# A one-core FFT filter plus gated MLP: the layout of the normalised rows, one low op for two, and ten opening pieces on GpSimd

## The chip, the cores and the metric

The kernel runs on one core of a Trainium2 chip. The metric is the device time of one execution in microseconds, given as the median of several runs. A separate profiled execution gives the trace.

## The reference

The input x has 2048 rows of 448 numbers. It is normalised row by row, and two branches of the normalised xn are added to x:

```python
xn = _layernorm(x, axis=-1)
return x + _A_ref(xn, A_w_r, A_w_i) + _B_ref(xn, B_W_gate, B_W_up, B_W_down)
...
# _A_ref: a filter in the frequency plane
X = rfft2(x) * (w_r + 1j * w_i);  y = irfft2(X, s=(S, D))
# _B_ref: a gated MLP with 1792 hidden units
gate = x @ W_gate;  up = x @ W_up;  gate = gate * (gate > 0)
return (gate * up) @ W_down
```

## The kernel before

**Numbers.** Every matmul operand is split into a float16 high half and a float16 low half (the value minus the high half). A product takes three passes: high by high, high by low, low by high. A "low op" is the subtraction that makes a low half; it reads two tensors of SBUF (the value and its high half).

**Rows.** The rows are taken as 16 tiles n2 = 0..15 of 128 rows. Four chunks q hold the tiles with n2 % 4 = q and are worked in the order 0, 2, 1, 3. A tile goes through these steps, and the opening calls them by these short names: `lx` loads it (L220), `st` takes its statistics on VectorE (L248, L251), `sq` and `rs` make the reciprocal deviation for a group of tiles (L259 to L273), `xn` normalises it in float32 on VectorE (L291), `hi` rounds it to float16 on ScalarE (L298 from x in chunk 0, L300 from xn in the others), `lo` subtracts (L320, L321), `cp` and `cl` make small copies inside the tile on GpSimd (L304 and L305 for the high half, L309 and L310 for the low half). The tile in SBUF is `tt`, nine blocks of 128 columns; there are four such buffers, taken in turn.

**Layout.** The columns of a row are split by their remainder mod 4 into three groups a, b, c (of 112, each filled up to 128 with 16 of the odd group) and d, the 64 odd columns left. In `tt` they stand as a, b, c, d high, then d, a, b, c low, then two blocks of copies that hold the whole odd group (48 + 16 zeros + 64) for the Fourier part, high and low.

**Transposition.** The blocks must be transposed into `T`. For chunk 0 TensorE does it (`tpA`, `tpB`, L335) and VectorE or ScalarE copies the result out of PSUM (`vevA`, `aevA` and so on, L343 and L341); block 8 alone goes by a DMA transpose (`dt`, L329). For chunk 2 whole tiles go by DMA transposes (`dm`, L329). All DMA issues named here stand in SyncE's queue.

**Weights.** A hidden slab f (128 units; 14 in three groups) has a gate and an up slab g = 0, 1. `lw` loads one (L226), `wsq` squares it on ScalarE (L186), `par` sums over partitions on GpSimd (L189), `wsc` makes a scale on VectorE (L192, L196), `whi` makes its high half on ScalarE (L665) and `wlo` its low half on VectorE (L669).

**MLP.** `gu` is one slab's passes over 512 rows (L715). The last d block needs only 64 rows of the array, so two slabs share four half passes, `hp` (L722). `re` and `tm` make relu and product from PSUM (L752 on ScalarE, L756 on VectorE), `gh` and `gl` split it (L760, L764). The down projection is L783. In chunk 0 slab 0 is split further into pieces `hh`, `lh`, `hl` by half of the rows, so that TensorE can start early. `kw` and `warm` are dummy matmuls (L1023).

**Order.** For the opening (the first 38 us or so) the order of all engines is written out by hand in the string `OPENING`: 230 pieces; each engine runs its own pieces in that order. It ends with the last slab of chunk 0 and `hp4`, the half passes that also open chunk 2. Behind it the order comes from a planner: background work is dealt out between the units of the MLP by costs written in the code, and the framework places the instructions.

Of the kernel before, what the change touches and what calls it, by code (L numbers as in the profile page):

```python
# [133 lines left out]
def tile_gfnet_reglu(ctx: ExitStack, tc: tile.TileContext, x, xr, wgu, wd, wf, wrow, ident, c_fd, c_fm, c_im, c_row, c_id,  # L134
                     out):
    nc = tc.nc
# [8 lines left out]
    def fx():  # L145
        return psum.tile([128, 512], F32, name="fx", bufs=2)
# [131 lines left out]
    xn, tt, xn_b = {}, {}, {}  # L278
    tts = [ft([128, 9, 128], F16, f"tt{i}") for i in range(4)]
    for t in tts:  # L280
        G.memset(t[:, 7:9, 48:64], 0.0)

    def new_tt(n2):
        tt[n2] = tts[state.setdefault("tn", 0) % 4]
        state["tn"] += 1

    def ln_xn(n2):
        xn_b[n2] = free.pop(0)
        xn[n2] = xn_b[n2].rearrange("p g c k -> p (g c k)")[:, 0:D]
        r, _, mean = rsn[n2 % 4, n2 // 4]  # L290
        V.tensor_scalar(xn[n2], xr_t[n2], mean, r, op0=OP.subtract, op1=OP.mult)  # L291

    def ln_hi(n2, fused=False):
        new_tt(n2)
        o = tt[n2].rearrange("p a b -> p (a b)")[:, 0:D]
        r, nm, _ = rsn[n2 % 4, n2 // 4]
        if fused:
            A.activation(o, xr_t[n2], AF.Identity, scale=r, bias=nm)  # L298
        else:
            A.activation(o, xn[n2], AF.Copy)  # L300

    def ln_copy(n2):
        t = tt[n2]
        G.tensor_copy(t[:, 7, 0:48].rearrange("p (a b) -> p a b", b=16), t[:, 0:3, 112:128])  # L304
        G.tensor_copy(t[:, 7, 64:128], t[:, 3, 0:64])  # L305

    def ln_copy_lo(n2):
        t = tt[n2]
        G.tensor_copy(t[:, 8, 0:48].rearrange("p (a b) -> p a b", b=16), t[:, 4:7, 112:128])  # L309
        G.tensor_copy(t[:, 8, 64:128], t[:, 3, 64:128])  # L310
# [6 lines left out]

    def ln_lo(n2):
        x, t = xn[n2], tt[n2].rearrange("p a b -> p (a b)")
        V.tensor_tensor(t[:, 512:896], x[:, 0:384], t[:, 0:384], op=OP.subtract)  # L320
        V.tensor_tensor(t[:, 448:512], x[:, 384:448], t[:, 384:448], op=OP.subtract)  # L321
        free.append(xn_b.pop(n2))

    tp, last = {}, {}

    def ln_dma(n2, a=0):
        q, j = n2 % 4, n2 // 4
        o = Tq[q][:, a:9, 128 * j:128 * (j + 1)]
        last["S"] = nc.sync.dma_start_transpose(o, tt[n2][:, a:9].rearrange("p a b -> p (a b)")).ins  # L329

    def ln_tp(n2, tiles):
        if n2 not in tp:
            tp[n2] = fx().bitcast(F16).rearrange("p (a b) -> p a b", b=128)
        for a in tiles:
            P.transpose(tp[n2][:, a, :], tt[n2][:, a, :], id_t)  # L335

    def ln_ev(n2, a0, a1, act):
        q, j = n2 % 4, n2 // 4
        o = Tq[q][:, a0:a1, 128 * j:128 * (j + 1)]
        if act:  # L340
            last["A"] = A.activation(o, tp[n2][:, a0:a1], AF.Copy).ins  # L341
        else:
            last["V"] = V.tensor_copy(o, tp[n2][:, a0:a1]).ins  # L343
# [359 lines left out]

    hps, ht = {}, {}

    SEQ = [(r + 4 * k, r) for r in range(3) for k in (0, 1)] + [(t, 4 + t) for t in range(3)] + [(3, 3)]
    TOP = ((slice(0, 64), 3), (slice(64, 128), 7))

    def gu_open(f, q):
        hps[f, q] = psum.tile([128, 2, 512], F32, name="gu", bufs=2)  # L710
# [44 lines left out]
        g1 = g1s[f, q]  # L755
        last["V"] = V.scalar_tensor_tensor(g1, hps[f, q][:, 1, :], 2.0 ** -22, g1, op0=OP.mult, op1=OP.mult).ins  # L756
# [443 lines left out]
```

## Time and profile before

| | |
|---|---|
| median of 3 runs | 446.72 us (446.71 to 446.97) |
| profiled execution | 446.92 us, span 445.1 us |
| TensorE busy | 438.4 us, 98% |
| VectorE busy | 373.5 us, 84% |
| ScalarE busy | 178.9 us, 40% |
| GpSimd busy | 32.9 us, 7% |
| granted TensorE clock | 1.00 in every stretch |

In the profile PE is TensorE's matmuls, PEld its weight loads, DVE VectorE, ACT ScalarE, POOL GpSimd, and SPq SyncE's queue that issues DMAs. A row of the timeline gives the start, the duration, the engine, the line, the operation, output and input, how many instructions are merged, and in brackets the idle time before it with what ended it. Instructions of one engine overlap by a little, so a step from start to start is shorter than the duration. Grouped rows give count, busy time and the mean in ns.

### The profile page before, as it was taken

To read this page: it belongs to the slowest core of one execution; us is meant where nothing else is said; L and a number is where in the kernel's file an instruction comes from. 1 tells how busy PE (TensorE), PEld (TensorE's weight loads), DVE (VectorE), ACT (ScalarE), POOL (GpSimd) and SP (SyncE) were. 2 spreads that over 40 slices of the span, in tenths; PEclk is the share of its full clock that TensorE was granted. 3 is DMA by queue.
4 is the path that set the end of the run, shared out by engine and by line. 5 is a ranking of instruction groups with operands and counts; after the bars stand their busy time and mean duration, and the time that the engine had idled before them with its cause. 6 is when DMAs were issued, how large, how long until landed. Compare 5 with 4: busy or idle time off the path is not lost.

```text
span 445.1 us, 7091 instructions
## 1 busy us (share of the span) xinstructions
PE 438.4 (98%) x2630; PEld 218.8 (49%) x2630; DVE 373.5 (84%) x802; ACT 178.9 (40%) x365; POOL 32.9 (7%) x97
## 2 busy tenths in 40 slices
PE   8999999999999999999999999999999999999997
PEld 3543554444546444444444444444444455556565
DVE  5988696998858979999999999896997997766364
ACT  5886252351543666043233145344142242233230
POOL 2431031040000120000000010000000000000000
DMA  8929966041001261432220021000001333231113
GB/s 271 323 52 282 371 217 119 1 90 41 0 14 61 95 222 34 133 105 62 85 80 6 1 84 55 0 13 0 14 0 42 93 96 90 55 96 34 63 43 124
DMA packets 37115, 39.72 MB, mean 89 GB/s; under 512 B 17927, under 2 KB 32473, under 8 KB 37081
## 3 DMA queue, kind: packets, MB, share of 16 engines
q1 hardware_dynamic: 35928, 37.40, 27.4%
q10 hardware_dynamic: 1152, 1.87, 2.1%
q8 instruction: 20, 0.33, 0.3%
q14 instruction: 15, 0.11, 0.1%
HBM read 24.45 MB, written 3.67 MB: 63 GB/s over the span
## 4 chain that ended last, share of the span: by engine, by line
PE 91%; DVE 3%; DMA 2%; ACT 1%; issue 1%; POOL 1%; SPq 0%; ACTq 0%
PE gu L715 50%; PE dn L783 29%; PE gu L722 3%; PE fx L611 2%; PE fx L357 2%; PE fx L632 2%; PE fx L389 2%; DMA y<-in_xr 1%; DMA T<-tt 1%; DVE bst L248 1%; DVE wt L669 1%; DVE y L291 0%; DVE g L756 0%; ACT T L341 0%; DVE tt L320 0%
## 5 line engine op out<-in xcount | busy, mean ns | idle before, releaser
L715 PE MATMUL gu<-T,wt 128*128 128x512 f16 (+1 forms) x1140 | 256.1, 375 | 0.0
L715 PEld LDWEIGHTS <-wt 128*128 128x128 f16 x1140 | 108.7, 98 | 129.8 <-issue 9.3
L783 PE MATMUL dn<-wdt,h 128*128 128x448 f16 (+2 forms) x684 | 136.4, 349 | 0.0
L783 PEld LDWEIGHTS <-h 128*128 128x128 f16 x684 | 65.8, 98 | 59.9
L752 ACT ACTIVATE g<-gu 128x512 f32<-128x512 f32 x56 | 33.2, 594 | 115.1 <-PE gu L722 77.4
L760 ACT ACTIVATE h<-g 128x512 f16<-128x512 f32 x56 | 35.0, 627 | 47.3 <-DVE g L756 47.3
L756 DVE SCALAR_TENSOR_TENSOR g<-gu,g 128x512 f32<-128x512 f32 x56 | 38.5, 687 | 11.4 <-ACT g L752 11.3
L790 DVE SCALAR_TENSOR_TENSOR xy<-dn,dsc,xy 128x448 f32<-128x448 f32 (+2 forms) x49 | 32.9, 671 | 15.1 <-PE dn L783 14.8
L764 DVE TENSOR_TENSOR h<-g,h 128x512 f16<-128x512 f32 x56 | 38.5, 689 | 4.9 <-ACT h L760 4.8
L665 ACT ACTIVATE wt<-wst,wsc 128x512 f16<-128x512 f32 x28 | 19.1, 716 | 15.7 <-DVE wsc L196 15.7
L669 DVE SCALAR_TENSOR_TENSOR wt<-wst,wsc,wt 128x512 f16<-128x512 f32 x28 | 20.5, 749 | 0.0
L637 DVE SCALAR_TENSOR_TENSOR xy<-fx,fsc,xy 128x448 f32<-128x448 f32 x16 | 10.8, 681 | 10.7 <-PE fx L632 10.7
L189 POOL PARTITION_ALL_REDUCE wm<-wm x15 | 7.8, 521 | 158.9 <-ACT junk L186 158.9
L396 DVE TENSOR_TENSOR y<-y 128x456 f32<-128x456 f32 x22 | 13.9, 631 | 4.8 <-DMA row<-y 4.5
L722 PE MATMUL gu<-T,wt 64*128 64x512 f16 x112 | 17.0, 381 | 0.8 <-DMA T<-tt 0.7
L186 ACT ACTIVATE junk<-wst 128x512 bf16<-128x512 f32 x28 | 17.4, 622 | 0.2
L595 ACT ACTIVATE vt<-y,fsc 128x912 f16<-128x912 f32 x8 | 8.4, 1052 | 20.7 <-PE fx L611 12.3
L618 ACT ACTIVATE wf<-fx 114x512 f16<-114x512 f32 x16 | 9.4, 588 | 17.4 <-PE fx L611 16.6
L553 DVE TENSOR_TENSOR y<-y,sw 128x456 f32<-128x456 f32 x16 | 10.1, 628 | 5.7 <-DMA sw<-y 5.7
L395 DVE TENSOR_TENSOR y<-y 128x456 f32<-128x456 f32 x22 | 13.8, 628 | 0.2
L611 PEld LDWEIGHTS <-vt 128*128 128x128 f16 x192 | 12.0, 98 | 3.3
L611 PE MATMUL fx<-wf,vt 128*128 128x128 f16 x192 | 13.2, 219 | 0.0
(115 smaller groups left out, 431.4 us busy)
## 6 DMA issues: line engine op xcount, KB each, us to landing
wst<-in_wgu SPq DMA_DIRECT2D x28, 256.0 KB
wf<-in_wf SPq DMA_DIRECT2D x8, 456.0 KB
sw<-y SPq DMA_DIRECT2D x16, 224.4 KB
y<-in_xr SPq DMA_DIRECT2D x16, 224.0 KB
xy<-in_x SPq DMA_DIRECT2D x16, 224.0 KB
out<-xy SPq DMA_DIRECT2D x15, 224.0 KB
wdst<-in_wd SPq DMA_DIRECT2D x14, 224.0 KB
sw<-y SPq DMA_DIRECT2D x8, 228.0 KB
```

Source lines behind the costliest of these rows:

```text
L186: A.activation(o, src, AF.Square, scale=SQ, accum_out=acc)
L611: P.matmul(o, v[:, h, w], m[:, c, :], start=(i == 0), stop=(i == 2), skip_group_check=True)
L665: A.activation(w[:, 0:4, :], wst[f, g], AF.Copy, scale=wsc[f, g])
L669: V.scalar_tensor_tensor(w[:, 4:8, :], st, sc, w[:, 0:4, :], op0=OP.mult, op1=OP.subtract)
L715: last["P"] = P.matmul(hps[f, q][:, g, cs], wt[f, g][:, a, :], Tq[q][:, b, cs], start=(start and i == 0), stop=(stop and i == len(seq) - 1 ...
L722: m = P.matmul(hps[f, q][:, g, 0:512], wt[f, g][rows, 7, :], Tq[q][rows, b, :], start=start, stop=not start).ins
L752: last["A"] = A.activation(g1s[f, q], hps[f, q][:, 0, :], AF.Relu, scale=2.0 ** -22).ins
L756: last["V"] = V.scalar_tensor_tensor(g1, hps[f, q][:, 1, :], 2.0 ** -22, g1, op0=OP.mult, op1=OP.mult).ins
L760: A.activation(ht[f, q][:, 0, :], g1s[f, q], AF.Copy)
L764: V.tensor_tensor(h[:, 1, :], g1s.pop((f, q)), h[:, 0, :], op=OP.subtract)
L783: last["P"] = P.matmul(ps[:, 0:c1 - c0], ht[f, q][:, a, js], wdt[f][:, b, c0:c1], start=(i == 0), stop=(i == n - 1)).ins
L790: last["V"] = V.scalar_tensor_tensor(o, dps[n2][:, 0:c1 - c0], dsc[:, g:g + 1], o, op0=OP.mult, op1=OP.add).ins
```

## The change

The layout becomes [odd columns, d, a, b, c], once high (blocks 0 to 3) and once low (blocks 4 to 7). So `hi` writes columns 64 to 512 and `lo` is one op on 576 to 1024. Block 8 becomes the pair (d high, d low) that the half passes and the d pass need. In chunk 0 it is not copied: two half transposes of TensorE put it together in PSUM, and `cp` and `cl` are one copy each there, not two; in the other chunks they are two as before. Both evacuations of a tile are now 512 columns (they were 384 and 640). `dt` transposes block 4. The host lays the columns of x to match. The matmuls of the MLP and of the Fourier part are the same in number and read other blocks.

Ten pieces of the opening go to GpSimd: `px4`, `px12`, `px2` (xn), `pwhiW0g0`, `pwhiW1g1`, `pwhiW2g1`, `pwhiW3g1` (whi), `phi2`, `phi6` (hi) and `pgh4` (gh). One evacuation moves from ScalarE to VectorE (`vevA8`). The pieces stand in another order, the loads too.

```diff
 OPENING = """
-lx0 lx4 lw lid lw lx8 lx12 lw lw lw lw lx2 lx10 lx6 lx14 lwd0 lwd1 lwd2 lwd3 lwd4 warm st0 st4 sqA rsA.0 rsA.1 rsA.2 rsA.3 rsA.4 hi4 xn4 xn0 wsqW0g0 cp4 st8 hi0 parW0g0 st12 wsqW0g1 cp0 tpA0 lo0 tpA4 kw1 wscW0g0.0 wscW0g0.1 sqB tpB0 kw6 parW0g1 wsqW1g0 rsB.0 rsB.1 rsB.2 rsB.3 rsB.4 whiW0g0 vevB0 lo4 wsqW1g1 xn12 tpB4 kw3 hi8 parW1 wscW0g1.0 wscW0g1.1 xn8 whiW0g1 cp8 vevA0 vevA4 hi12 tpA8 vevB4 hh10 hh00 lo8 wsqW2g1 cp12 tpA12 hl00 lo12 aevA12 tpB8 aevA8 hl10 wloW0g0 lw aevB8 tpB12 wscW1.0 wscW1.1 lh00 aevB12 wloW0g1 lw lfd hh01 hh11 whiW1g0 st2 lh01 lh10 whiW1g1 hl01 wloW1g0 lw hl11 wsqW2g0 cl0 cl4 wloW1g1 lw ly0 ly4 ly8 ly12 lh11 wsqW3g0 st10 parW2 hp0 st14 wsqW3g1 gu1g0 st6 wdq0 parW3 cl8 cl12 wscW2.0 wscW2.1 sqC wscW3.0 wscW3.1 whiW2g0 rsC.0 rsC.1 rsC.2 rsC.3 gu1g1 re0 wloW2g0 whiW3g1 tm0 whiW2g1 xn6 wsqW4g0 xn2 gu2g0 dt0 dt4 wloW2g1 hi2 dt8 dt12 re1 xn10 gh0 wloW3g1 whiW3g0 tm1 gu2g1 wdq1 wloW3g0 hi10 xn14 lo2 hi14 hi6 cp14 hp2 wsqW4g1 cp2 lo6 gu3g0 cp10 cl2 dm2 lo14 re2 parW4 wdq2 cp6 wscW4.0 wscW4.1 tm2 whiW4g0 cl14 dm14 lo10 wdq4 gu3g1 wloW4g0 gh1 cl10 dm10 gl0 whiW4g1 gl1 cl6 dm6 gu4g0 re3 wloW4g1 wdq3 tm3 wdp gh3 wdsc gh2 gu4g1 gl2 wdh1 wdh2 wdl1 wdh0 wdl2 hp4 gl3 re4 wdh3 tm4 wdl0 gh4 wdh4 gl4 wdl3 wdl4
+lx0 lx4 lw lx12 lw lx8 lw lid lw lx2 lw lw lx10 lw lx6 lx14 lwd4 lwd1 warm st0 st4 sqA rsA.0 rsA.1 rsA.2 rsA.3 rsA.4 st12 wsqW0g0 hi4 xn0 st8 hi0 wsqW0g1 px4 cp4 parW0g0 parW0g1 cp0 lo0 sqB kw6 tpA0 tpB0 kw1 tpA4 wsqW1g0 rsB.0 wscW0g1.0 wscW0g0.0 wscW0g1.1 rsB.1 wscW0g0.1 lo4 rsB.2 vevB0 rsB.3 vevA0 rsB.4 tpB4 kw3 whiW0g1 wsqW1g1 hi8 vevA4 xn8 pwhiW0g0 px12 hi12 lo8 vevB4 hh10 hh00 cp8 tpA8 wsqW2g1 parW1 cp12 cl0 tpB8 tpA12 hl00 hl10 lo12 wscW1.0 aevA12 tpB12 vevA8 wscW1.1 wloW0g0 whiW1g0 aevB8 aevB12 wloW0g1 hh11 wloW1g0 lh01 lh00 lh11 lh10 hh01 hl01 hl11 wsqW2g0 cl12 pwhiW1g1 cl8 parW2 cl4 wloW1g1 ly4 lw lwd0 dt12 lw ly0 lwd2 ly8 dt0 lfd dt4 lwd3 dt8 lw ly12 wsqW3g0 wsqW3g1 hp0 st6 st14 st2 st10 wscW2.0 gu1g0 wdq0 parW3 sqC wscW2.1 rsC.0 wscW3.0 whiW2g0 gu1g1 re0 wscW3.1 rsC.1 rsC.2 rsC.3 wloW2g0 tm0 pwhiW2g1 wsqW4g0 whiW3g0 re1 xn6 wloW2g1 xn10 gu2g0 px2 pwhiW3g1 xn14 wloW3g1 wloW3g0 tm1 gu2g1 phi2 wdq1 hi10 wdq4 wsqW4g1 gh0 hi14 lo2 gh1 hp2 cp2 phi6 parW4 cp14 cl2 gu3g0 dm2 re2 lo14 lo10 wscW4.0 wscW4.1 lo6 gl0 tm2 whiW4g0 whiW4g1 wdq2 gh2 wdq3 cl14 cp6 cl10 cl6 cp10 gu3g1 wloW4g0 dm14 dm10 dm6 gu4g0 gl2 wloW4g1 re3 tm3 wdp wdsc gl1 gh3 gu4g1 hp4 wdh3 wdh0 wdh2 wdh1 re4 gl3 wdl3 wdl2 tm4 wdh4 pgh4 wdl1 wdl0 wdl4 gl4
 """
...
-    return np.concatenate([m + r for r in (0, 2, 1, 3)]), np.concatenate([*_rows()[:3], _rows()[3, :64]])
+    return np.concatenate([m + r for r in (0, 2, 1, 3)]), np.concatenate([_rows()[3, :64], *_rows()[:3]])
...
-    def ln_xn(n2):
+    def ln_xn(n2, e=V):
...
-        V.tensor_scalar(xn[n2], xr_t[n2], mean, r, op0=OP.subtract, op1=OP.mult)
+        e.tensor_scalar(xn[n2], xr_t[n2], mean, r, op0=OP.subtract, op1=OP.mult)
...
-        o = tt[n2].rearrange("p a b -> p (a b)")[:, 0:D]
+        o = tt[n2].rearrange("p a b -> p (a b)")[:, 64:64 + D]
...
+        elif e is G:
+            G.tensor_copy(o, xn[n2])
...
-        G.tensor_copy(t[:, 7, 0:48].rearrange("p (a b) -> p a b", b=16), t[:, 0:3, 112:128])
-        G.tensor_copy(t[:, 7, 64:128], t[:, 3, 0:64])
+        G.tensor_copy(t[:, 0, 0:48].rearrange("p (a b) -> p a b", b=16), t[:, 1:4, 112:128])
+        if n2 % 4 != CHUNKS[0]:
+            G.tensor_copy(t[:, 8, 0:64], t[:, 0, 64:128])
...
-        V.tensor_tensor(t[:, 512:896], x[:, 0:384], t[:, 0:384], op=OP.subtract)
-        V.tensor_tensor(t[:, 448:512], x[:, 384:448], t[:, 384:448], op=OP.subtract)
+        V.tensor_tensor(t[:, 576:1024], x, t[:, 64:512], op=OP.subtract)
...
+            o = tp[n2][:, a - a // 5, :]
+            if a < 8:
+                P.transpose(o, t[:, a, :], id_t)
+            else:
+                P.transpose(o[0:64], t[:, 0, 64:128], id_t)
+                P.transpose(o[64:128], t[:, 4, 64:128], id_t)
...
-    def w_hi(f, g):
+    def w_hi(f, g, e=A):
...
+        if e is G:
+            G.tensor_scalar(w[:, 0:4, :], wst[f, g], wsc[f, g], None, op0=OP.mult)
...
-    SEQ = [(r + 4 * k, r) for r in range(3) for k in (0, 1)] + [(t, 4 + t) for t in range(3)] + [(3, 3)]
-    TOP = ((slice(0, 64), 3), (slice(64, 128), 7))
+    SEQ = [(r + 4 * k, 1 + r) for r in range(3) for k in (0, 1)] + [(t, 5 + t) for t in range(4)]
+    TOP = ((slice(0, 64), 8), (slice(64, 128), 0))
```

More of the change, by code (lines that the diff above doesn't have):

```diff
@@ L280, in tile_gfnet_reglu @@
     for t in tts:
[L281 removed]
+        G.memset(t[:, 0:5:4, 48:64], 0.0)
     def new_tt(n2):
@@ L290, in ln_xn, with ln_hi @@
         r, _, mean = rsn[n2 % 4, n2 // 4]
[L291 to L293 removed]
+        e.tensor_scalar(xn[n2], xr_t[n2], mean, r, op0=OP.subtract, op1=OP.mult)
+    def ln_hi(n2, fused=False, e=A):
         new_tt(n2)
[L295 removed]
+        o = tt[n2].rearrange("p a b -> p (a b)")[:, 64:64 + D]
         r, nm, _ = rsn[n2 % 4, n2 // 4]
[L297 removed]
+        if e is G and fused:
+            G.tensor_scalar(o, xr_t[n2], r, nm, op0=OP.mult, op1=OP.add)
+        elif e is G:
+            G.tensor_copy(o, xn[n2])
+        elif fused:
             A.activation(o, xr_t[n2], AF.Identity, scale=r, bias=nm)
@@ L333, in ln_tp, with ln_ev @@
             tp[n2] = fx().bitcast(F16).rearrange("p (a b) -> p a b", b=128)
+        t = tt[n2]
         for a in tiles:
-            P.transpose(tp[n2][:, a, :], tt[n2][:, a, :], id_t)
-    def ln_ev(n2, a0, a1, act):
+            o = tp[n2][:, a - a // 5, :]
[4 more added lines that the diff above has]
+                P.transpose(o[64:128], t[:, 4, 64:128], id_t)
+    def ln_ev(n2, b, act):
         q, j = n2 % 4, n2 // 4
-        o = Tq[q][:, a0:a1, 128 * j:128 * (j + 1)]
+        o = Tq[q][:, 5 * b:4 + 5 * b, 128 * j:128 * (j + 1)]
+        i = tp[n2][:, 4 * b:4 + 4 * b]
         if act:
-            last["A"] = A.activation(o, tp[n2][:, a0:a1], AF.Copy).ins
+            last["A"] = A.activation(o, i, AF.Copy).ins
         else:
-            last["V"] = V.tensor_copy(o, tp[n2][:, a0:a1]).ins
+            last["V"] = V.tensor_copy(o, i).ins
     zps, eo, X, Xh, yps, cur = {}, {}, {}, {}, {}, {}
@@ L661, in w_scale @@
             wsc[f, k] = sc[:, i:i + 1]
-    def w_hi(f, g):
+    def w_hi(f, g, e=A):
         w = wt[f, g] = mt([128, 8, 128], F16, "wt", 2 * NR + 4)
-        A.activation(w[:, 0:4, :], wst[f, g], AF.Copy, scale=wsc[f, g])
+        if e is G:
+            G.tensor_scalar(w[:, 0:4, :], wst[f, g], wsc[f, g], None, op0=OP.mult)
+        else:
+            A.activation(w[:, 0:4, :], wst[f, g], AF.Copy, scale=wsc[f, g])
     def w_lo(f, g):
@@ L1017, in tile_gfnet_reglu @@
     half = (slice(0, 256), slice(256, 512))
-    seq1 = [(r + 4 * k, r) for k in (0, 1) for r in range(3)]
-    seq2 = [(r, r + 4) for r in range(3)] + [(3, 3)]
+    seq1 = [(r + 4 * k, 1 + r) for k in (0, 1) for r in range(3)]
+    seq2 = [(r, 5 + r) for r in range(4)]
     def keep_warm(n):
@@ L1064, in tile_gfnet_reglu @@
             piece(f"{tag}{f}", fn, f, q)
+        piece(f"pgh{f}", gu_hi, f, q, G)
         if f % 2 == 0:
@@ L1069, in tile_gfnet_reglu @@
             piece(f"whiW{f}g{g}", w_hi, f, g)
+            piece(f"pwhiW{f}g{g}", w_hi, f, g, G)
             piece(f"wloW{f}g{g}", w_lo, f, g)
```

30 lines of the change are left out of this document (17 added, 13 removed).

## The prediction

> **What bounds the kernel now.** I read the profile's page first, then the busy time by stage, then TensorE's own timeline, then the chain that ended last.
>
> ```profile
> span 445.1 us, 7091 instructions
> ...
> PE 438.4 (98%) x2630; PEld 218.8 (49%) x2630; DVE 373.5 (84%) x802; ACT 178.9 (40%) x365; POOL 32.9 (7%) x97
> ```
> ```profile
> 13.00:19.00 6.00, 5.53 (x56) 4.74 (x56) 5.89 (x16) 5.74 (x13) 2.12 (x7) 1.00 0.98 327
> 19.00:28.40 9.40, 9.24 (x45) 3.95 (x44) 9.13 (x26) 8.71 (x21) 1.47 (x6) 1.00 0.45 131
> 28.40:38.60 10.20, 9.57 (x45) 3.87 (x44) 8.64 (x28) 7.98 (x19) 5.70 (x18) 1.00 0.67 125
> 38.60:60.00 21.40, 21.35 (x145) 11.69 (x146) 16.88 (x41) 7.44 (x15) 0.00 (x0) 1.00 1.03 366
> 60.00:442.00 382.00, 382.00 (x2297) 190.39 (x2295) 324.26 (x662) 141.42 (x285) 20.12 (x49) 1.00 0.21 61
> ```
> The columns after the stretch and its length are PE, PEld, DVE, ACT and POOL busy, then the granted clock. From 38.6 us to 442 TensorE does not stop, at full clock. Nothing that the change does there can shorten the run unless it removes matmuls, and it removes none. Before 38.6 it is VectorE and ScalarE that are full (13 to 19: 5.89 and 5.74 of 6.00). So the whole question is when TensorE gets past 38.65:
>
> ```profile
> 19.17 0.61 PE L722 MATMUL gu<-T,wt 64*128 64x512 f16 x4 [0.15 <-DVE wt L669]
> 28.98 8.99 PE L715 MATMUL gu<-T,wt 128*128 128x512 f16 x40
> 38.65 0.61 PE L722 MATMUL gu<-T,wt 64*128 64x512 f16 x4 [0.68 <-DMA T<-tt]
> ```
> ```profile
> 35.27 3.25 DMA T<-tt
> ```
> The L722 rows are the pieces hp0 and hp4. hp4 opens chunk 2. It needs two things: TensorE through with chunk 0 (28.98 + 8.99 = 37.97), and the transposed chunk 2, whose last transfer lands at 38.52 (35.27 + 3.25, a link of the chain). I call them gate A and gate B. The kernel gains only as much as the later of the two moves.
>
> **Prices.** VectorE steps are taken from start to start:
>
> ```profile
> 8.42 0.63 DVE L248 BATCH_NORM_STATS2 bst<-y 128x6 f32<-128x448 f32 x1
> 9.18 0.54 DVE L320 TENSOR_TENSOR tt<-y,tt 128x384 f16<-128x384 f32 x1
> 9.64 0.21 DVE L321 TENSOR_TENSOR tt<-y,tt 128x64 f16<-128x64 f32 x1
> 9.78 0.14 DVE L192 TENSOR_SCALAR eg<-wm 128x1 uint32<-128x1 uint32 x1
> 17.70 1.42 DVE L669 SCALAR_TENSOR_TENSOR wt<-wst,wsc,wt 128x512 f16<-128x512 f32 x2
> 23.15 0.68 DVE L756 SCALAR_TENSOR_TENSOR g<-gu,g 128x512 f32<-128x512 f32 x1
> 23.75 0.93 DVE L291 TENSOR_SCALAR y<-y,mv,rs 128x448 f32<-128x448 f32 x2
> ```
> ```profile
> L669 DVE SCALAR_TENSOR_TENSOR wt<-wst,wsc,wt 128x512 f16<-128x512 f32 x10 | 7.4, 749 | 0.0
> L291 DVE TENSOR_SCALAR y<-y,mv,rs 128x448 f32<-128x448 f32 x8 | 3.9, 508 | 0.0
> L343 DVE COPY T<-fx 128x640 f16<-128x640 f16 x2 | 1.0, 484 | 0.0
> L343 DVE COPY T<-fx 128x384 f16<-128x384 f16 x2 | 0.6, 350 | 0.0
> ```
> A pair of statistics (st) is 0.76 (8.42 to 9.18). The low half (lo) is 0.46 + 0.14 = 0.60 now; one op of 448 is 0.46 x 448/384 = 0.54, so the merge saves 0.06 apiece. A low weight slab (wlo) is 1.42 - 0.75 = 0.67, an xn 0.93 - 0.51 = 0.42, a product (tm) 23.75 - 23.15 = 0.60. An evacuation of 512 columns lies between those of 384 and 640; less the overlap of 0.08 that the other rows show, about 0.33.
>
> No row has a GpSimd op of 448 or 512 elements with an input. The nearest:
>
> ```profile
> 0.96 0.52 POOL L1083 MEMSET warm<- 128x512 f16 x1
> 28.90 0.22 POOL L304 COPY tt<-tt 128x48 f16<-128x48 f16 x1 [7.34 <-ACT tt L300]
> 29.06 0.24 POOL L305 COPY tt<-tt 128x64 f16<-128x64 f16 x1
> 29.24 0.22 POOL L304 COPY tt<-tt 128x48 f16<-128x48 f16 x1
> 33.04 0.70 POOL L310 COPY tt<-tt 128x64 f16<-128x64 f16 x1
> 33.69 0.68 POOL L309 COPY tt<-tt 128x48 f16<-128x48 f16 x1
> 34.31 0.70 POOL L310 COPY tt<-tt 128x64 f16<-128x64 f16 x1
> ```
> ```profile
> 32.87 0.78 DVE L669 SCALAR_TENSOR_TENSOR wt<-wst,wsc,wt 128x512 f16<-128x512 f32 x1
> 33.57 1.35 DVE L764 TENSOR_TENSOR h<-g,h 128x512 f16<-128x512 f32 x2
> ```
> A write of 512 elements is 0.52 (lower end). A copy of 64 is 0.24, 0.02 over one of 48, about 1 ns an element; 0.24 + 448 ns = 0.69 (upper end from these rows). I take 0.65 for each of the ten pieces. The last three copies show the other cost: 0.70 instead of 0.24, each ending just after a VectorE op with two SBUF inputs ends (32.87 + 0.78 = 33.65; the copy ends at 33.74). So a copy costs a step of 0.17 when free and 0.65 when held. The Trainium skill states this as an exclusive lock (SBUF — State Buffer, "Who interferes with whom": such an op and a GpSimd op that reads SBUF block each other, whichever comes second); the rows show it for copies behind VectorE, and no row here shows it the other way round. Its GPSIMD Engine Reference (§3.1) gives 769 ns for a measured loop over 512 elements. At that price each piece would cost 0.12 more and the sum below would come out about 0.2 later.
>
> **Gate A, the four half passes hp0 at 19.17.** hp0 waits for the last wlo, which ends VectorE's unbroken stretch from 7.61:
>
> ```profile
> 7.61 0.63 DVE L248 BATCH_NORM_STATS2 bst<-y 128x6 f32<-128x448 f32 x1 [0.40 <-DMA y<-in_xr]
> 5.00:10.00 5.00, 4.42 (x23) 1.80 (x22) 4.00 (x16) 3.63 (x9) 1.56 (x6) 1.00 1.00 354
> y<-in_xr SPq DMA_DIRECT2D x16, 224.0 KB
> wst<-in_wgu SPq DMA_DIRECT2D x18, 256.0 KB
> id_t<-in_ident SPq DMA_DIRECT2D x1, 32.0 KB
> ```
> The new order starts that stretch with st12. lx12 is now the fourth load: 3 x 224 + 256 = 928 KB up to its end, where lx8 needed 1216 KB for its landing at 7.6. 288 KB at 354 GB/s is 0.8, so st12 starts at 6.8. lx8 (1408 KB) lands 192 KB or 0.55 after 7.6, and VectorE, done with st12 and xn0 at 8.0, waits 0.15 for it. In the stretch xn12 (0.42), st2 (0.76) and 4 x 0.06 go; xn0 (0.42, earlier in front of it) and the evacuation vevA8 (0.33) come: -0.67. xn4 leaves VectorE too, but it lay in front of the wait at 7.61. The four added transposes lie under the same stretch and cost nothing; were TensorE the limit there, each would cost at most what a 512-column matmul does (8.99 / 40 = 0.22). End: 19.12 - 0.8 + 0.15 - 0.67 = 17.8. The piece pwhiW1g1 stands among the four wlo and can hold one of them for up to 0.65; I add half. hp0 at 18.1, 1.05 earlier. Behind hp0 TensorE needs 18.80 (19.17 to 37.97). In it is one wait that should go, since wloW4g0 comes earlier:
>
> ```profile
> PEld L715 <- DVE wt L669: 0.5, 1, 0.5
> ```
> A new one comes, because all four st now stand between the last wlo and tm0, and gu2g0 needs the PSUM that tm0 frees. VectorE: 18.1, four st (3.05), ten small ops of 0.14 at most (1.3), wloW2g0 (0.67), tm0 (0.68): 23.8 at the latest, 23.6 if the small ops overlap. TensorE is there after hp0 (0.61) and 20 matmuls of 0.22: 23.2. The wait of about 0.5 cancels the one that goes. Gate A comes at 18.1 + 18.8 = 36.9, 1.05 earlier.
>
> **Gate B, chunk 2.** In order on GpSimd: pwhiW2g1, px2, pwhiW3g1, phi2, cp2, phi6, parW4, then 14 copies for the four tiles. The four st and the small ops end on VectorE about 22.4, and the five pieces (5 x 0.65, with one or two steps held by a wlo) follow: done by about 26.7. The 14 copies must also wait for hi14:
>
> ```profile
> 28.26 1.04 ACT L300 ACTIVATE tt<-y 128x448 f16<-128x448 f32 x2 [0.28 <-DVE y L291]
> ```
> These are hi14 and hi6. In the new order three ScalarE ops in front of hi14 go to GpSimd (whiW2g1, whiW3g1, hi2), two squares are moved in front of it, so one step of about 0.5 is saved beside the 1.05 of hp0, which starts this chain: hi14 from 26.7 to 27.3, or half a us later if ScalarE waits for xn14. So the pieces have about 0.8 us of cover; without it each 0.1 on their price would cost 0.5. On VectorE, after tm0 (about 23.6), stand 3 xn, 3 wlo, tm1, 4 lo and two small ops: 1.26 + 2.0 + 0.6 + 2.16 + 0.3 = 6.3, so the last lo ends at 29.9. Four copies follow it: 30.6 if free. If each of the six two-input ops around them holds one (0.48 more each), cp10 ends at about 33.1. What comes then is SyncE's:
>
> ```profile
> 31.01 5.59 SPq L329 DMA_TRANSPOSE T<-tt  x4
> ```
> One transpose takes 1.40 of its queue and lands 3.25 after its issue. cp10, now last on GpSimd, releases dm10, the last but one: + 1.4 + 3.25 + 0.1. That makes 35.3 to 37.8; the queue itself, with dm2 at about 29, allows no less than 29 + 3 x 1.4 + 3.25 = 36.5. I take 37.4, toward the upper end, as the rows at 33.04 to 34.31 show every copy held. This is against 38.52 now.
>
> So gate B still decides, hp4 comes at 37.5, 1.15 earlier. The 406.4 behind it stays: the same matmuls, and the eight merged lo there lie under a TensorE without idle time (0.5 in all if they did not). The profiled execution took 446.92 for its span of 445.1; it becomes 445.8. Its median was 446.72, so I forecast **445.6**.
>
> **Rivals.**
> - *The lock turns round.* A VectorE op with two inputs that comes during a piece waits for it. Five pieces among wlo and lo of chunk 2 could hold VectorE by up to 5 x 0.65 = 3.2; with 2.9 the last lo ends at 32.8, and even free copies bring 32.8 + 0.7 + 4.75 = 38.25. Time 446.4 to 446.7, no change. (This is the rule of SBUF — State Buffer in the Trainium skill, applied to the pieces.) For it: the held copies. Against it: the VectorE ops at 33.57 average 0.68 each although copies stood between them.
> - *GpSimd becomes the bound (slower).* If a piece costs more than about 1 us, five in a row use up the cover of 0.8 and the gain of 1.15 (0.65 + 1.95/5 = 1.04 is the turning point). At 1.3 gate B falls 5 x 0.26 = 1.3 behind where it is now, time 448.0. For it: POOL does no such op anywhere in this trace. Against: 0.52 for 512 written elements.
> - *TensorE decides.* If the copies run free, gate B is 36.5 and A's 36.9 counts: 446.72 - 1.75 = 445.0. For it: the free steps of 0.16 at 28.90. Against: the held ones later.
> - *The planned part shifts.* Behind the opening the planner orders by its own costs; an op at a wrong place stops TensorE for one VectorE step or so, 0.7, and the gain halves to 446.3. Nothing in the trace shows such a stop now.
> - *The change does not do what it says*: the merged lo costs as much as two. That is 0.25 at gate A, which does not decide.
>
> **How the numbers follow.** About 0.2% (0.9 us) is what a measurement of this kernel can tell from no change; faster means under 445.83. Forecast 0.50 (445.1 to 446.1, so a fifth of it within 0.2%), TensorE decides 0.12, lock turned round 0.18, planner 0.06, slower 0.14 (a little of it within 0.2%). Faster 0.52, same 0.35, slower 0.13. The range is 444.8 (both gates free and no piece held at gate A, 17.8 instead of 18.1) to 447.0, which leaves most of the GpSimd case out.
>
> **What would show it.** Right: hp0 at about 18, hp4 at 37 to 38 still released by DMA T<-tt, GpSimd ops of 448 and 512 at 0.5 to 0.7, st12 at 6.8. Wrong: pieces over 1 us; wlo or lo much longer than 0.75 and 0.62; hp4 at 38.5 or later; TensorE idle behind 40.

## The result and the profile after

| | before | after |
|---|---|---|
| median of 5 runs | 446.72 us (446.46 to 447.00) | 492.15 us (491.32 to 492.71) |
| profiled execution | 446.92 us, span 445.1 | 492.57 us, span 490.8 |
| hp0 (the first half passes) | 19.17 | 47.29 |
| hp4 (opens chunk 2) | 38.65 | 84.31 |

The change makes the kernel slower: the ratio is 1.101, with a 95% interval of 1.0997 to 1.1027. The forecast was faster by 1.1 us. All of the loss, 45.4 us, lies where the prediction looked, before hp4: 84.31 - 38.65 = 45.7.

```profile
47.29 0.61 PE L737 MATMUL gu<-T,wt 64*128 64x512 f16 x4 [3.35 <-DVE wt L684]
...
84.31 0.60 PE L737 MATMUL gu<-T,wt 64*128 64x512 f16 x4
```

The page of the kernel after shows it in its 40 slices of 12.3 us each: TensorE is idle for large parts of the first seven, and the granted clock falls there. Then both are as before.

```profile
PE 451.1 (92%) x2634; PEld 222.6 (45%) x2634; DVE 373.5 (76%) x784; ACT 174.7 (36%) x357; POOL 44.3 (9%) x99
...
PE   6316587999999999999999999999999999999997
...
POOL 2022154022030001200000000000000000000000
PEclk9567877999999999999999999999999999999999
```

The busy time by stretch (columns as in the prediction) shows that no engine is the bound there. From 13 to 19 us not one of them has an instruction running; from 19 to 38.6 the DMA engines move nothing either (the last two columns are their share and GB/s). An opening that was full on VectorE and ScalarE now stands still for long stretches, and no engine's work accounts for them.

```profile
13.00:19.00 6.00, 0.00 (x0) 0.00 (x0) 0.00 (x0) 0.00 (x0) 0.00 (x0) 0.60 0.51 189
19.00:28.40 9.40, 4.40 (x25) 2.38 (x25) 3.77 (x15) 3.36 (x7) 2.00 (x4) 0.68 0.00 0
28.40:38.60 10.20, 3.06 (x20) 1.96 (x21) 1.89 (x6) 0.42 (x1) 3.44 (x7) 0.50 0.00 0
100.00:442.00 342.00, 342.00 (x1934) 165.28 (x1933) 301.57 (x630) 128.97 (x267) 19.28 (x49) 1.00 0.23 65
```

GpSimd's own timeline names it. Here are its tensor_scalar pieces and all-reduces up to hp4, with one cast:

```profile
9.91 1.88 POOL L291 TENSOR_SCALAR y<-y,mv,rs 128x448 f32<-128x448 f32 x1 [8.42 <-DMA wst<-in_wgu]
...
19.60 0.77 POOL L189 PARTITION_ALL_REDUCE wm<-wm  x2 [7.62 <-issue]
...
27.33 1.57 POOL L678 TENSOR_SCALAR wt<-wst,wsc 128x512 f16<-128x512 f32 x1 [6.80 <-issue]
...
36.90 0.41 POOL L189 PARTITION_ALL_REDUCE wm<-wm  x1 [5.95 <-issue]
...
44.88 1.57 POOL L678 TENSOR_SCALAR wt<-wst,wsc 128x512 f16<-128x512 f32 x1 [7.07 <-issue]
...
52.39 0.41 POOL L189 PARTITION_ALL_REDUCE wm<-wm  x1 [5.76 <-issue]
...
60.44 1.57 POOL L678 TENSOR_SCALAR wt<-wst,wsc 128x512 f16<-128x512 f32 x1 [7.08 <-issue]
...
65.52 0.55 POOL L300 CAST tt<-y 128x448 f16<-128x448 f32 x1
...
74.20 0.40 POOL L189 PARTITION_ALL_REDUCE wm<-wm  x1 [6.33 <-issue]
```

Each time GpSimd goes from a tensor_scalar to an all-reduce, or back, 5.8 to 7.6 us go by in which it waits for nothing that the profile shows ("issue"). There are seven such changes, and an eighth gap in front of the first tensor_scalar. Between two operations of the same kind there is no gap, and copies and casts run on either side without one. The first gap is put down to a DMA that this operation does not read; one of the experiments below (e3) shows its operands there by 6.14, and here it starts at 9.91. The waits of GpSimd sum the other seven:

```profile
POOL wm L189 <- issue: 25.7, 4, 7.6
POOL wt L678 <- issue: 21.0, 3, 7.1
```

Everything else hangs on these. The low halves on VectorE need the high half of the same slab, so VectorE waits for line 678. The scales need the all-reduce, so ScalarE and VectorE wait for line 189. The copies of the tiles stand behind both in GpSimd's order. And TensorE waits for all of them.

### The profile page after: what moved, and what is told of

It is laid out like the page before. It is cut to its first block, busy times and chain, and to the rows that moved or that the text cites. A ratio compares the mean times of both kernels' runs of the same rounds, so it can differ in the third digit from the quotient of the medians.

```text
span 490.8 us, 7085 instructions
## 1 busy us (share of the span) xinstructions
PE 451.1 (92%) x2634; PEld 222.6 (45%) x2634; DVE 373.5 (76%) x784; ACT 174.7 (36%) x357; POOL 44.3 (9%) x99
## 4 chain that ended last, share of the span: by engine, by line
PE 84%; issue 7%; POOL 3%; DVE 2%; DMA 2%; ACT 0%; SPq 0%; POOLq 0%; DVEq 0%
PE gu L730 47%; PE dn L801 26%; PE gu L737 3%; PE fx L623 2%; PE fx L369 2%; PE fx L644 2%; PE fx L401 2%; DMA wst<-in_wgu 2%; POOL wt L678 1%; POOL y L291 1%; DVE wt L684 0%; DVE bst L248 0%; POOL wm L189 0%; DVE g L771 0%; PE fx L343 0%
## 5 line engine op out<-in xcount | busy, mean ns | idle before, releaser
L730 PE MATMUL gu<-T,wt 128*128 128x512 f16 (+1 forms) x1140 | 264.9, 384 | 14.2 <-POOL wt L678 7.8
L730 PEld LDWEIGHTS <-wt 128*128 128x128 f16 x1140 | 110.7, 100 | 151.5 <-issue 20.5
L680 ACT ACTIVATE wt<-wst,wsc 128x512 f16<-128x512 f32 x24 | 16.3, 713 | 33.4 <-DVE wsc L196 33.4
L192 DVE TENSOR_SCALAR eg<-wm 128x2 uint32<-128x2 uint32 (+1 forms) x15 | 2.3, 159 | 24.9 <-POOL wm L189 24.8
L343 PE MATMUL fx<-id_t,tt 128*128 128x128 f16 x28 | 3.9, 311 | 17.2 <-POOL tt L308 17.2
L607 ACT ACTIVATE vt<-y,fsc 128x912 f16<-128x912 f32 x8 | 8.4, 1052 | 20.7 <-PE fx L623 12.3
L630 ACT ACTIVATE wf<-fx 114x512 f16<-114x512 f32 x16 | 9.4, 588 | 17.8 <-PE fx L623 17.0
L326 DVE TENSOR_TENSOR tt<-y,tt 128x448 f16<-128x448 f32 x16 | 9.6, 626 | 5.6 <-POOL y L291 5.5
```

Source lines behind the costliest of these rows:

```text
L730: last["P"] = P.matmul(hps[f, q][:, g, cs], wt[f, g][:, a, :], Tq[q][:, b, cs], start=(start and i == 0), stop=(stop and i == len(seq) - 1 ...
```

## The experiments

**Theory S**: a change between tensor_scalar and all-reduce costs 5.8 to 7.6 us, since GpSimd must bring in another program, and the eight gaps are the loss. **Theory L**, the rival: tensor_scalar is long (1.57 to 1.88 here) and the pieces and VectorE's two-input operations hold each other up, and that is the loss. The kernel before had a median of 446.89 us beside e1 to e4, 447.07 beside e5 to e8 and 446.85 beside e9 and e10.

**e1: the seven tensor_scalar pieces back to VectorE and ScalarE.** The three casts (`phi2`, `phi6`, `pgh4`), the layout and the new order stay.

The pieces keep their names and places; only their engine changes.

```diff
-            for tag, fn, *a in (("lx", load_xr), ("ly", load_x), ("st", ln_stats, j), ("xn", ln_xn), ("px", ln_xn, G),
+            for tag, fn, *a in (("lx", load_xr), ("ly", load_x), ("st", ln_stats, j), ("xn", ln_xn), ("px", ln_xn),
...
-            piece(f"pwhiW{f}g{g}", w_hi, f, g, G)
+            piece(f"pwhiW{f}g{g}", w_hi, f, g)
```

> The seven tensor_scalar pieces (px4, px12, px2 and the four pwhi) go back to VectorE and ScalarE at the same places of the new order; phi2, phi6 and pgh4 stay on GpSimd, and so does the new layout. Theory S (switching GpSimd between the program of its tensor_scalar and that of its all-reduce costs 5 to 7.5 us each time, and that is the whole loss): no stretch of GpSimd without work of over 3 us in front of an op that is ready, TensorE's clock back at 1.00, time 445.5 to 449. Theory O (the new order or the new layout stalls by itself): 455 or more. Theory L (long GpSimd ops hold VectorE by the shared lock): also about 446 to 449, so this run does not part S from L.

Measured: 449.71 us (448.72 to 450.79), ratio 1.006 (1.0048 to 1.0078). So 42.4 of the 45.4 us hang on these seven pieces, as theory S has it (theory L too). But 2.8 us over before are left, which S alone doesn't explain. TensorE is through with chunk 0 at 29.58 + 8.81 = 38.39, but hp4 comes only at 40.95, held by the transposed tiles:

```profile
29.58 8.81 PE L730 MATMUL gu<-T,wt 128*128 128x512 f16 x40
40.95 0.61 PE L737 MATMUL gu<-T,wt 64*128 64x512 f16 x4 [2.56 <-DMA T<-tt]
```

**e2: the layout alone.** The old order of the pieces, nothing new on GpSimd, `vevA8` back on ScalarE.

```diff
 OPENING = """
-lx0 lx4 lw lx12 lw lx8 lw lid ...
+lx0 lx4 lw lid lw lx8 lx12 lw ...
```

> The new layout (one low op, block 8 built by TensorE in chunk 0, 512-column evacuations) with the order of before and nothing more on GpSimd. S and L: 446.0 to 447.0, the merged low op worth 0 to 0.7 us. O, if it is the layout that stalls: 450 or more.

Measured: 448.11 us (447.73 to 448.55), ratio 1.0027 (1.0017 to 1.0037). This is over what was expected: the layout, which the prediction costed at a small gain, costs 1.2 us. It shows at gate B, here in the last four low copies, the transposes and hp4:

```profile
33.60 0.68 POOL L314 COPY tt<-tt 128x48 f16<-128x48 f16 x1 [0.92 <-DVE tt L326]
...
35.49 0.73 POOL L316 COPY tt<-tt 128x64 f16<-128x64 f16 x1
```
```profile
31.65 6.03 SPq L334 DMA_TRANSPOSE T<-tt  x4
```
```profile
39.80 0.61 PE L737 MATMUL gu<-T,wt 64*128 64x512 f16 x4 [1.27 <-DMA T<-tt]
```

The two copies between took 0.70 and 0.68. In before the last three of the four took 0.70, 0.68 and 0.70 too, but not the first:

```profile
32.88 0.22 POOL L309 COPY tt<-tt 128x48 f16<-128x48 f16 x1 [0.85 <-DVE tt L320]
```

It was released by the first of the two low ops (line 320) and ran beside the second, a short one. With one merged op the copy is released by the end of all of it and meets the next two-input operation on VectorE: 0.68. So the merge, which was priced at 0.06 saved on VectorE, costs a copy 0.46. The first transpose is issued 0.64 later than in before, and the four take 6.03 in place of 5.59. If the costs add up, these 1.2 us are part of the 2.8 that e1 left over; the other 1.6 then come with the new order and the three casts, which no run takes apart.

**e3: the all-reduces left out.** Every sum over partitions becomes a copy, so the scales of the weights and of the Fourier part are left uncomputed; the ten pieces stay as the change has them.

```diff
-        G.partition_all_reduce(o, i, 128, bass_isa.ReduceOp.add)
+        G.tensor_copy(o, i)
```

> The changed kernel with every sum over partitions left out: the all-reduce becomes a GpSimd copy of the same few numbers. The ten pieces stay on GpSimd. S: no switch is left but the first load, so the stretches of 5 to 7.5 us in front of the all-reduces and of the tensor_scalar pieces go, and seven of the pieces still take 1.6 to 1.9 us: 449 to 457. L: the pieces and their collisions are all still there, so 480 or more.

Measured, in one run: 449.22 us. With no all-reduce beside the tensor_scalar on GpSimd the gaps are gone, though the pieces are as long as in the kernel after or longer:

```profile
6.14 1.91 POOL L291 TENSOR_SCALAR y<-y,mv,rs 128x448 f32<-128x448 f32 x1 [4.65 <-DVE rs L271]
...
15.33 2.58 POOL L678 TENSOR_SCALAR wt<-wst,wsc 128x512 f16<-128x512 f32 x1 [0.42 <-DVE wsc L196]
...
21.98 1.59 POOL L678 TENSOR_SCALAR wt<-wst,wsc 128x512 f16<-128x512 f32 x1 [2.36 <-DVE wsc L196]
23.57 2.37 POOL L291 TENSOR_SCALAR y<-y,mv,rs 128x448 f32<-128x448 f32 x1
25.91 1.82 POOL L678 TENSOR_SCALAR wt<-wst,wsc 128x512 f16<-128x512 f32 x1
```
```profile
40.97 0.61 PE L737 MATMUL gu<-T,wt 64*128 64x512 f16 x4 [1.51 <-DMA T<-tt]
```

hp4 comes at 40.97, not 84.31: the eight gaps are 43.3 us, 5.4 apiece. Theory L falls as the main cause. Long pieces and the layout together cost what is left, 40.97 - 38.65 = 2.3.

**e4: the seven pieces as copies.** The same number of elements, but a plain copy or cast; the all-reduces stay. Left out are the normalisation of tiles 4, 12 and 2 and the scaling of four high halves.

```diff
-        e.tensor_scalar(xn[n2], xr_t[n2], mean, r, op0=OP.subtract, op1=OP.mult)
+        if e is G:
+            G.tensor_copy(xn[n2], xr_t[n2])
...
-            G.tensor_scalar(w[:, 0:4, :], wst[f, g], wsc[f, g], None, op0=OP.mult)
+            G.tensor_copy(w[:, 0:4, :], wst[f, g])
```

> The changed kernel with the seven tensor_scalar pieces as plain GpSimd copies or casts of the same size; the normalisation of tiles 4, 12 and 2 and the scaling of four weight halves are left out. All-reduces stay. S: a copy needs no other program, so no switch at all, and a piece takes 0.5 to 0.7 us as the two casts in the trace of the change do (0.55): this is the kernel that the prediction had in mind, 445.0 to 447.0. L: collisions stay, 450 or more.

Measured: 447.83 us (447.65 to 449.23), ratio 1.0028 (1.0017 to 1.0039). This is the kernel that the prediction had priced: pieces of about 0.65 and nothing between them. It too is slower than before, by 0.9 us, which was not expected. Against e1, with the same layout and order and the seven pieces on VectorE and ScalarE, it is 1.9 us faster: at such a price the move to GpSimd gains, and the layout with the new order loses more. Rows of GpSimd and VectorE at one place, of GpSimd's last copy, of TensorE, and of the transposes:

```profile
9.51 0.61 POOL L681 CAST wt<-wst 128x512 f16<-128x512 f32 x1
10.07 0.56 POOL L292 COPY y<-y 128x448 f32<-128x448 f32 x1
...
34.49 0.23 POOL L313 COPY tt<-tt 128x64 f16<-128x64 f16 x1
```
```profile
10.12 0.98 DVE L329 TENSOR_TENSOR tt<-y,tt 128x448 f16<-128x448 f32 x1
```
```profile
18.69 0.60 PE L740 MATMUL gu<-T,wt 64*128 64x512 f16 x4
...
24.39 4.48 PE L733 MATMUL gu<-T,wt 128*128 128x512 f16 x20 [0.68 <-DVE g L774]
...
39.57 0.61 PE L740 MATMUL gu<-T,wt 64*128 64x512 f16 x4 [1.42 <-DVE wdt L719]
```
```profile
30.73 6.75 SPq L337 DMA_TRANSPOSE T<-tt  x4
```

hp4's row names a VectorE operation of line 719, which ended just before it. That is a piece `wdl`, which stands behind hp4 in the order, so hp4 cannot need it; what it needs is the last transpose, which lands at about 39.4 (worked out below).

A low op that begins while GpSimd reads (10.12, beside the copy at 10.07) takes 0.98, not 0.6: the hold works in this direction as well. And the four transposes take 6.75, since the last copies end at 34.72 and not at 33.1.

**e5: one tensor_scalar piece alone, in the kernel before.**

```diff
-        A.activation(w[:, 0:4, :], wst[f, g], AF.Copy, scale=wsc[f, g])
+        if (f, g) == (2, 1):
+            G.tensor_scalar(w[:, 0:4, :], wst[f, g], wsc[f, g], None, op0=OP.mult)
+        else:
+            A.activation(w[:, 0:4, :], wst[f, g], AF.Copy, scale=wsc[f, g])
```

> The kernel before with one piece moved: the high half of weight slab (2,1) is a tensor_scalar on GpSimd, nothing else changes. Theory S (each change between tensor_scalar and the all-reduce costs 5.4 to 7.4 us): two changes. The piece starts about 28 instead of 23.5 and takes 1.57; gu2g1, due at 26.5, stalls by about 3.3. The all-reduce of slab 4, at 30.96 in before, comes about 38; slab 4's weights are ready at 40, and the copies behind the all-reduce, so dm14, dm10 and dm6, come after 38.4, the last landing about 45.4. hp4 at 45 to 46 (before 38.65), time 452 to 455. Theory L (the long pieces and the shared access to SBUF made most of the loss): one piece of 1.57 in place of a ScalarE op of 0.5, hp4 at most 1 to 2 later, time 447 to 449, and no gap without work around the all-reduce.

Measured: 459.67 us (459.14 to 460.20), ratio 1.028 (1.0263 to 1.0301). One piece of 1.57 us costs 12.6:

```profile
28.81 1.57 POOL L666 TENSOR_SCALAR wt<-wst,wsc 128x512 f16<-128x512 f32 x1 [7.41 <-issue]
...
36.54 0.23 POOL L310 COPY tt<-tt 128x64 f16<-128x64 f16 x1
42.86 0.41 POOL L189 PARTITION_ALL_REDUCE wm<-wm  x1 [6.09 <-issue]
```
```profile
30.44 0.61 PE L718 MATMUL gu<-T,wt 128*128 128x512 f16 x1 [4.24 <-POOL wt L666]
31.22 4.02 PE L718 MATMUL gu<-T,wt 128*128 128x512 f16 x9 [0.18 <-DVE wt L672]
...
44.62 0.61 PE L718 MATMUL gu<-T,wt 128*128 128x512 f16 x1 [3.98 <-ACT wt L668]
...
51.92 0.61 PE L725 MATMUL gu<-T,wt 64*128 64x512 f16 x4
```
```profile
28.40:38.60 10.20, 7.98 (x26) 2.58 (x27) 5.52 (x12) 3.38 (x8) 3.67 (x9) 0.67 0.06 12
```

The mechanism is theory S's; its size was too small, for two reasons that the rows show. The second gap does not begin when the piece is done (30.4) but when the all-reduce's turn comes in GpSimd's order, behind the copies that end at 36.77. So the all-reduce is at 42.86, not at 38. And after TensorE has stood still, its granted clock is 0.67, and nine matmuls take 4.02 (0.45 each, where 40 took 8.99, 0.22 each).

**e9: the same piece as a tensor_tensor.**

```diff
-            G.tensor_scalar(w[:, 0:4, :], wst[f, g], wsc[f, g], None, op0=OP.mult)
+            G.tensor_tensor(w[:, 0:4, :], wst[f, g], wsc[f, g].to_broadcast([128, 4, 128]), op=OP.mult)
```

> As e5, one high half (slab 2,1) on GpSimd, but as a tensor_tensor with the scale read again for every element, not as a tensor_scalar. Theory P (any arithmetic operation with a scalar or second operand needs another program than the all-reduce on GpSimd; copies, casts and memsets do not): the same two gaps of 6 to 7.4 us as in e5, time 457 to 461. Rival Q (only the tensor_scalar needs it): no gap, the operation starts about 23.5 and takes 1 to 2 us, hp4 at most 1 later, time 447 to 448.5.

Measured: 459.99 us, ratio 1.029 (1.0272 to 1.0310).

```profile
29.13 1.03 POOL L666 TENSOR_TENSOR wt<-wst,wsc 128x512 f16<-128x512 f32 x1 [7.67 <-issue]
...
42.71 0.41 POOL L189 PARTITION_ALL_REDUCE wm<-wm  x1 [6.16 <-issue]
```

The same two gaps. So it is not the one operation: what does arithmetic here (tensor_scalar, tensor_tensor) needs the change, what moves or rounds (copy, cast, memset) does not. Theory P holds for the kinds tried.

**e6, e7, e8, e10: are the two gates real?** If hp4 waits for the later of two gates, moving gate B alone must gain up to gate A and no more. e6 is the kernel before with chunk 2 in another order: the copies of tile 2 first, its transpose at once, then tiles 6, 14, 10.

```diff
-... hi10 xn14 lo2 hi14 hi6 cp14 hp2 wsqW4g1 cp2 lo6 gu3g0 cp10 cl2 dm2 lo14 re2 parW4 wdq2 cp6 wscW4.0 wscW4.1 tm2 whiW4g0 cl14 dm14 lo10 wdq4 gu3g1 wloW4g0 gh1 cl10 dm10 gl0 whiW4g1 gl1 cl6 dm6 gu4g0 ...
+... hi10 xn14 cp2 lo2 cl2 dm2 hi14 hi6 hp2 wsqW4g1 lo6 cp14 gu3g0 cp6 cl6 dm6 cp10 lo14 re2 lo10 parW4 wdq2 cl14 dm14 cl10 dm10 wscW4.0 wscW4.1 tm2 whiW4g0 wdq4 gu3g1 wloW4g0 gh1 gl0 whiW4g1 gl1 gu4g0 ...
```

> The kernel before with another order of the copies and transposes of chunk 2 only: cp2 and cl2 first, then tiles 6, 14, 10; lo10 right behind lo14. Theory G (gate B, the last transposed tile at 38.52, decides, with TensorE's gate A at 37.97 next): dm2 is issued about 29.4 instead of 31.01, the last transfer lands 36.9 to 37.3, hp4 follows TensorE at 38.0 to 38.2, time 446.1 to 446.4, 0.5 less than before. Rival (the order on VectorE is what binds: lo10 in front of tm2 holds the PSUM of gu4): hp4 at 38.5 or later, no gain.

Measured: 446.54 us (445.97 to 447.23), ratio 0.9988 (0.9979 to 0.9997).

```profile
29.28 5.93 SPq L329 DMA_TRANSPOSE T<-tt  x4
```
```profile
34.05 4.27 PE L715 MATMUL gu<-T,wt 128*128 128x512 f16 x19 [0.26 <-DVE wt L669]
38.26 0.60 PE L722 MATMUL gu<-T,wt 64*128 64x512 f16 x4
```

The transposes start 1.73 earlier, the wait for T<-tt is gone, and hp4 follows TensorE's own work at 38.26. The gain is 0.5, as far as gate A allows. The rival, that lo10 would hold the products, did not come about.

e7 is the layout-only kernel e2 with the same new order.

> The layout-only kernel of e2 with the same new order of copies and transposes as e6. Theory G: the 1.2 us that the layout cost lies only in the chain of copies and transposes of chunk 2, which now has slack; hp4 at 38.0 to 38.4, time 446.2 to 446.7, the same as e6 within 0.3. Rival (the layout costs TensorE something else, such as the later hp0, 19.36 for 19.17, or the planned part): 447 or more.

Measured: 447.12 us (446.75 to 447.39), ratio 1.0001 (0.9992 to 1.0010); hp0 at 19.42, hp4 at 38.97 without a wait for T<-tt. Gate B is out of the way here as well, and the layout still costs 447.12 - 446.54 = 0.6. So about half of its 1.2 lay at gate B. The other half is spread over gate A: 0.15 up to hp0, 0.21 from there to the next half passes, 0.35 from these to hp4. (The first of these is within what one execution differs from another: with the same pieces in front, hp0 comes at 19.17 in before, 19.27 in e6, 18.85 in e8 and 19.41 in e10.) The expectation, the same as e6 within 0.3, missed. One thing the trace does show: with the shorter low ops VectorE is free for the third low half of a weight at 17.28, where e6 is at 17.79, but then it waits 0.63 for the high half from ScalarE, whose first evacuation had itself waited 0.50 for TensorE's transposition. So what the merge saves VectorE does not reach hp0. The rest is not settled.

e8 is e6 with one low half ahead of the second product split.

```diff
-... gl0 whiW4g1 gl1 gu4g0 re3 wloW4g1 ...
+... gl0 whiW4g1 wloW4g1 gl1 gu4g0 re3 ...
```

> e6 and also the low half of slab (4,1) on VectorE ahead of the second product split gl1. Theory G: the wait of TensorE for a low half (0.5, the only one in before) goes, gate A comes at 37.5 to 37.9, hp4 with it, time 445.6 to 446.1. Rival: that wait is for the other slab or is only covered by another, time as e6.

Measured: 446.48 us (446.00 to 447.06), ratio 0.9987 (0.9978 to 0.9995), the same as e6. In the profiled execution hp4 comes at 37.84, but far behind the opening, in the planned part, TensorE stands once:

```profile
114.16 4.48 PE L715 MATMUL gu<-T,wt 128*128 128x512 f16 x20 [0.79 <-DVE g L756]
```

That is what the prediction's rival of the shifting planned part describes, in another kernel: a gain in the opening given back later by one product. It is seen in this one execution, the slowest of e8's eleven (447.06); whether the others have it is not shown. Its hp0 was 0.42 earlier than e6's with the same pieces in front of it, and from hp0 to hp4 both take 18.99. So the moved low half gave nothing: the wait for a low half is still 0.26.

e10 is e6 with the all-reduce of slab 4 two steps earlier on GpSimd and its scale steps right behind lo14, since in e6 VectorE stood idle from 31.57 to 32.08 for that all-reduce.

```diff
-... cp6 cl6 dm6 cp10 lo14 re2 lo10 parW4 wdq2 cl14 dm14 cl10 dm10 wscW4.0 wscW4.1 tm2 whiW4g0 ...
+... cp6 parW4 cl6 dm6 cp10 lo14 re2 wscW4.0 wscW4.1 lo10 whiW4g0 wdq2 cl14 dm14 cl10 dm10 tm2 ...
```

> e6 and also the all-reduce of slab 4 ahead of cl6 and cp10, with the two scale steps right behind lo14. In e6 VectorE stood idle from 31.57 to 32.08 for that all-reduce and TensorE then waited 0.26 for a low half. Theory G (with gate B out of the way TensorE's gate A decides): hp4 at 37.6 to 38.0 in place of 38.26, time 446.0 to 446.5. Rival (as in e8 an earlier hp4 meets a later wait for a product on VectorE, line 756): hp4 earlier, time the same as e6 or more.

Measured: 446.03 us (445.81 to 446.25), ratio 0.9979 (0.9970 to 0.9988): 0.8 us less than before, the fastest kernel of this study. From hp2 to hp4 TensorE has no wait left:

```profile
28.69 0.61 PE L722 MATMUL gu<-T,wt 64*128 64x512 f16 x4
29.23 8.81 PE L715 MATMUL gu<-T,wt 128*128 128x512 f16 x40
37.97 0.61 PE L722 MATMUL gu<-T,wt 64*128 64x512 f16 x4
```

## Why the prediction was wrong

**The step that failed** is the price of the pieces: "No row has a GpSimd op of 448 or 512 elements with an input. The nearest: ... I take 0.65 for each of the ten pieces." The memset and the copies bounded the operation's own time, and nothing bounded what GpSimd does between an all-reduce and an operation of another kind. The kernel before has GpSimd do only copies, memsets and all-reduces, so its trace has no row of such a change, and the sum had no term for it. The term is 5.4 us for each of eight gaps (e3), 6.6 us for each of two, with the slower clock behind them (e5: hp4 later by 13.3). Worth noting is that the order string alone gave the count: the pieces in it alternate px4; two par; pwhi, px12; par; pwhi; two par; pwhi, px2, pwhi; par. These are eight groups with seven changes between them.

The Trainium skill has the rule, and the prediction passed over it: GPSIMD Engine Reference, "Instruction dispatch", says that GpSimd's operations are programs that can be loaded while the kernel runs, and that the first call after a load pays about 6 us with no instruction to be seen in the profile. The gaps here agree in size: three of the seven are 5.76, 5.95 and 6.33, the others 6.80 to 7.62. That a gap is such a load is taken from the page, as the trace shows only the idle time. The page does not say which operations share a program; e3, e4, e5 and e9 show it for the kinds tried.

**The own time of a piece.** For copies and casts it was right: eight of the ten in e4 took 0.56 to 0.69, the other two 0.95 (`phi6`) and 1.00 (`pgh4`, behind hp4). For tensor_scalar it was 1.57 (512 elements, one step) and 1.88 (448, two steps), 2.4 and 2.9 times the value taken and far over the upper bound of 0.69. A copy is no bound for an operation with arithmetic. VectorE does the same 448 elements in 0.51 (the group of line 291 in the prediction).

**The slower rival** had the right engine and the wrong reason. That GpSimd becomes the bound if a piece costs more than about 1 us fits what is left once the gaps are taken away: in e3 the five pieces of chunk 2 take 1.59, 2.37, 1.82, 0.55 and 0.56, 1.38 on average. By the rival's own sum that is 446.72 + 5 x (1.38 - 1.04) = 448.4; measured were 449.2, of which the layout has a share (e2). The real loss of 45.4 is eighteen times those 2.5.

**Gate A** was wrong even at the right price (e4). st12 starts at 6.91 (predicted 6.8). VectorE's last low half ends at 15.22 + 2.77 = 17.99 (17.8). But hp0 comes at 18.69 (18.1) with no wait in front of it: TensorE, with its four added transposes, was itself the last. It is busy for 5.92 of the 6 us from 13 to 19, where before it was 5.53, so "cost nothing" was wrong there; how much of the delay the four make is not measured by itself. The new wait for tm0 came (0.68; about 0.5 predicted), but it does not cancel against the wait that goes: that one was a wait of the weight loads, and the 40 matmuls behind the second half passes take 8.81 without it and 8.99 with it. TensorE is through at 38.15, against 36.9 predicted and 37.97 before.

**Gate B** was mis-sized most. Predicted 37.4; in e4 the last transpose is issued at 30.73 + 6.75 - 1.33 = 36.15, and with the 3.25 of before it lands at 39.4, later than in before. GpSimd is through with the five pieces at 25.84 (26.7 predicted); what it waits for is ScalarE: hi14 ends at 29.06, not 27.3; the copies behind it start at 29.12, the first two held (0.68 and 0.64), and dm2 is issued at 30.73, not 29. The layout takes 0.46 by the late release of a copy (e2), and a low op lasts 0.98, not 0.62, where GpSimd reads beside it (e4). So the rival of the lock that turns round is shown at single operations, with a smaller sum than it was given. Two sums come out otherwise by their own terms, without changing the reading: ten small operations of 0.14 are 1.4, not 1.3, and six holds of 0.48 behind 30.6 end at 33.5, not 33.1.

**What held.** That only the time up to hp4 counts, that two gates decide it, and that TensorE stays full behind it (the one execution of e8 apart). Gate B taken away by order alone gains 0.5 (e6), and taking away the wait on gate A as well gains 0.8 (e10); the engines do the same work in both. Of the forecast's 1.1 us, 0.8 was there to be had, but without the layout and without any piece on GpSimd.

## What to carry to other kernels

Before moving an operation to an engine, look in the trace for that operation on that engine. If no row has it, its own time is not the only unknown: what the engine must do to get from its present operations to the new one is another, and it is paid once for each alternation, so count the alternations in the engine's order. In these runs copies, casts and memsets on GpSimd mix with an all-reduce at no such cost; tensor_scalar and tensor_tensor pay it at each alternation, so keep them together or elsewhere. And when two releases are merged into one (here two low ops), ask who was waiting for the first.

## What the runs showed of the hardware

- A change between arithmetic and all-reduce on GpSimd costs 5.8 to 7.7 us of that engine's time (seven times in the kernel after, twice in e5 and in e9). In e5 the second one starts only when the all-reduce's turn comes, behind the copies that end at 36.77, although the piece was done at 30.4.
- The gap shows no DMA traffic (0 GB/s from 19 to 38.6 in the kernel after, over two such gaps) and no instruction that counts as busy; it shows only as idle time released by "issue".
- The first operation of its kind may or may not pay: the first all-reduce of the kernel before does not, nor the first tensor_scalar of e3, but the first tensor_scalar of the kernel after does. This fits a program that stays from the execution before, which ended with an all-reduce in the kernel after and with a tensor_scalar in e3. That was not tested by itself.
- tensor_scalar on 512 float32 elements takes 1.57 us on GpSimd where nothing holds it, tensor_tensor with the scalar read again for each element 1.03, a cast 0.61 to 0.69 (e4). The Trainium skill (GPSIMD Engine Reference, "Engine selection") has one-input operations at roughly line rate and two-input ones about twice as slow as on VectorE; here the one-input tensor_scalar is the slower of the two, and the measurement decides.
- TensorE's granted clock was 0.50 to 0.68 in the three stretches of the kernel after, shown above, in which it stood for much of the time or all of it, and 0.67 in that of e5; a matmul of 512 columns took 0.45 in e5 where it takes 0.22 at full clock. So part of the price of a stall is paid after it.
